# Wider triangle inversions on GpSimd, norms on VectorE, dummy matmuls and a new order in a fused gated-delta-rule kernel

## The chip, the cores and the metric

The kernel runs on one core of one Trainium2 chip. The metric is the time of one execution on the device, in microseconds (us). Executions of one kernel on one chip scatter here by about 3% (35 runs of the kernel before on one chip took 290.6 to 300.0 us; over all chips it took 289 to 303), so each kernel was timed in turn with the kernel before on the same chip. A ratio below is the mean time of one kernel's fast runs over that of the other's fast runs in the same rounds, with a 95% interval; it isn't quite the ratio of the medians that are quoted beside it. A run counts as slow when it lies over 1.5% above the fastest run of its kernel. With a scatter of 3% this cuts off the upper part of the scatter, and more of it the more runs there are. So where few runs are left, the ratio over all runs is given too.

Engine names in the profile: PE is TensorE, PEld its weight loads, DVE is VectorE, ACT is ScalarE, POOL is GpSimd, SP issues the loads.

## The reference, cut to what matters

```python
k_n = k / (np.linalg.norm(k, axis=-1, keepdims=True) + 1e-06)
for t in range(768):                       # for each of 4 x 8 heads, state 48 x 48
    y[t]  = g[t] * (q[t] @ state)
    state = state + beta[t] * outer(k_n[t], v[t] - k_n[t] @ state)
x = y                                      # 3072 tokens x 384
out = softplus(x @ w_in) @ w_out           # 384 -> 2048 -> 384
```

The recurrence is computed in chunks of 64 tokens. Within a chunk a unit lower triangle, made from the Gram products of the keys, is inverted and applied to (v - k state); the state passes from chunk to chunk. The dense part is two large matrix products with a softplus between them.

## The kernel before

Six steps, 0 to 5, of 128 tokens, each of two halves of 64. A small planner in Python puts every operation ("item") into the queue of its engine, which works it off in order (in run e13 below a transpose whose triangle had ended near 187 us started at 204.09, behind what stood ahead of it in VectorE's queue). The planner simulates the engines with a fixed duration for each item and, among the items that could start, takes the one with the best priority. Those priorities are a tuned table. So the order of each engine's queue is fixed before the kernel runs.

```python
class Plan:
    BLOCK = 128                 # matmuls
    FETCH = 3.5
    BUSY = {"POOL": 8.5, "ACT": 2.3, "DVE": 2.5}
    ...
            it = min(can, key=lambda x: (x.prio, x.n))
```

The triangle, 16 wide: two 16x16 triangles per lane, eliminated step by step, on VectorE in steps 0 and 1, on GpSimd from step 2 on:

```python
def step(j, ...):
    n, w = 15 - j, j + 1
    t = tmp[:, : 2*n*w]
    eng.tensor_tensor(t, nn[:, :, j+1:, j:j+1].broadcast_to([P, 2, n, w]),
                         tt[:, :, j:j+1, 16:16+w].broadcast_to([P, 2, n, w]), ALU.mult)
    rows = tt[:, :, j+1:, 16:16+w]
    eng.tensor_tensor(rows, rows, t, ALU.add)
...
for j in range(15): prev = add(en, 2*fix + 4*per*(15-j)*(j+1), lambda f=step, j=j: f(j), ...)
```

TensorE joins the 16x16 blocks to 32x32 by two products for each half, called the first and second cross product below (`xmm`, 64 matmuls, and `tmm`, 68), makes a lower-left block (`zmm`, 34) and applies the inverse in two parts (`umm`, 64, then after a copy `zu`, 32). The norms of steps 2 to 5 are a power on GpSimd:

```python
i3 = add("POOL", 5.6, lambda: nc.gpsimd.tensor_tensor(ss, ss, half_c, ALU.pow), ...)
```

## Time and profile before

| | before |
|---|---|
| median, 4 runs beside the changed kernel | 292.1 us (289.3 to 295.0) |
| span of the profiled run, mean granted clock of TensorE | 294.1 us, 0.932 |
| TensorE busy | 235.3 us, so 58.8 us idle |
| GpSimd: triangle of step 3 | 132.8 to 145.9 us |
| GpSimd: triangle of step 4 | 185.2 to 198.9 us |
| first cross product of step 0; first matmul of the dense layer | 34.6 us; 57.6 us |

The lines of the page that carry this are in the prediction below. Its "chain of waits" is the profile's path back from the last instruction, at each step to what that one waited for; the shares say which engine the end hung on, and "issue" is time in which an engine waited for nothing that the profile shows. The profiled run (295.8 us) lay 1.8% above the fastest of three timed runs, so it was labelled slow; each run has the span of one core only, so there is nothing to compare it with, and it serves for the places of things, not for ratios. One more view of the kernel before is needed later. Its columns are the stretch in us, its length, then the busy time (and number of instructions) of PE, PEld, DVE, ACT and POOL, the granted clock, the DMA share and GB/s:

```profile
120.00:140.00 20.00, 19.96 (x477) 10.60 (x476) 10.43 (x19) 13.78 (x26) 7.16 (x19) 0.80 0.93 148
160.00:180.00 20.00, 14.77 (x422) 8.05 (x421) 6.51 (x15) 9.65 (x20) 3.84 (x5) 0.91 1.22 136
```

TensorE is full from 120 to 140 us and waits for five of the twenty microseconds after 160.

Three more figures of this run, for the prediction. The granted clock is 0.50 from 124.6 to 127.5 us, where six dense matmuls took 2.74 us, and 1.00 from 128.7 to 130.3 us, where the same six took 1.47; from 57.6 to 60.3 us twelve smaller ones took 2.74 us at a granted clock of 1.00, and why is not shown. A multiply of 126 elements in the elimination takes 423 ns on GpSimd and 288 on VectorE, in the mean. And the page counts 50 packets on its instruction queue, 0.82 MB, for 6432 matmuls with a weight load each: 129 matmuls to a packet. The texts on record speak of blocks of instructions, of fetch and of instruction supply; a block is 128 matmuls there, and what the runs show of it stands under "The place of the boundaries".

### The profile page before, as it was taken

The numbers are of one execution on the slowest core, as the hardware profiler recorded it, in microseconds if no ns is written. First come the engines' busy times: TensorE is split into PE (matmuls) and PEld (weight loads), VectorE is DVE, ScalarE is ACT, GpSimd is POOL, SyncE is SP. The second block draws the span as 40 slices with busy tenths as digits, with TensorE's granted clock in tenths as the row PEclk, the third lists the DMA queues.
The fourth block names the chain that finished last, engine by engine and source line by source line (L and its number), as shares of the span: only waits on it lengthen the run. The fifth ranks groups of instructions, "written<-read, shape, count | busy, mean of one in ns | idle before, by whom it ended". The sixth has DMA issues, their size and how long they took to land.

```text
span 294.1 us, 14010 instructions
## 1 busy us (share of the span) xinstructions
PE 235.3 (80%) x6432; PEld 152.2 (52%) x6432; DVE 147.5 (50%) x290; ACT 140.4 (48%) x235; POOL 102.8 (35%) x182
## 2 busy tenths in 40 slices
PE   0365256696898985999798869999699999999993
PEld 0244145565656763455455535655455655667661
DVE  2899968657424891356465247475235601332110
ACT  3468545348426443577236527119534447513340
POOL 8443111714077840018877020880582000000000
PEclk9999999999589997589899979999779999999998
DMA  8999999999919999799979994884001320022112
GB/s 114 157 148 168 183 169 162 152 180 179 143 30 161 160 119 149 140 159 139 148 165 147 140 122 86 150 138 101 4 4 30 85 56 4 2 56 57 29 27 54
DMA packets 125931, 32.46 MB, mean 110 GB/s; under 512 B 119856, under 2 KB 125104, under 8 KB 125872
## 3 DMA queue, kind: packets, MB, share of 16 engines
q1 hardware_dynamic: 122752, 28.32, 63.2%
q0 software_dynamic: 3120, 3.24, 6.9%
q8 instruction: 50, 0.82, 1.2%
q14 instruction: 9, 0.07, 0.1%
HBM read 25.26 MB, written 4.72 MB: 102 GB/s over the span
## 4 chain that ended last, share of the span: by engine, by line
PE 68%; DVE 12%; issue 8%; ACT 5%; DMA 5%; SPq 0%; DVEq 0%; ACTq 0%
PE h L1341 25%; PE o L1379 20%; DMA kf<-in_k_dram 4%; PE d L1059 3%; PE d L1117 2%; PE d L1209 2%; PE d L970 2%; PE d L1015 2%; PE d L925 2%; PE d L1154 2%; ACT td L899 2%; PE d L1199 2%; DVE tt L835 1%; PE d L724 1%; DVE tmp L828 1%
## 5 line engine op out<-in xcount | busy, mean ns | idle before, releaser
L1362 ACT ACTIVATE ga<-h 128x512 f16<-128x512 f32 x96 | 57.2, 598 | 57.0 <-PE h L1341 55.0
L1341 PE MATMUL h<-xt,w_in 128*128 128x512 f16 (+1 forms) x384 | 81.8, 357 | 2.0 <-issue 2.0
L1379 PE MATMUL o<-w_out,ga 128*128 128x384 f16 x384 | 73.2, 337 | 1.3 <-DVE osb L1401 1.2
L1341 PEld LDWEIGHTS <-w_in 128*128 128x128 f16 x384 | 36.9, 104 | 25.7 <-issue 7.2
L1379 PEld LDWEIGHTS <-ga 128*128 128x128 f16 x384 | 36.6, 100 | 26.1 <-issue 4.4
L551 DVE CAST u<-d 128x384 f16<-128x384 f32 x24 | 13.4, 556 | 44.5 <-PE d L1117 25.1
L1401 DVE COPY osb<-o 128x384 f32<-128x384 f32 x24 | 13.3, 554 | 40.9 <-PE o L1379 38.6
L485 POOL TENSOR_TENSOR ss<-ss,half_c 128x32 f32<-128x32 f32 x4 | 21.8, 5448 | 10.8 <-DVE ss L448 7.6
L835 POOL TENSOR_TENSOR tt<-tt,tmp 128x30 f32<-128x30 f32 (+7 forms) x60 | 22.7, 378 | 4.7
L828 POOL TENSOR_TENSOR tmp<-nn,tt 128x30 f32<-128x30 f32 (+7 forms) x60 | 21.9, 365 | 4.5
L817 POOL TENSOR_TENSOR nn<-ln,beta_l 128x256 f32<-128x256 f16 x8 | 4.8, 618 | 50.3 <-DVE ln L793 50.3
L529 POOL CAST qn<-qf 128x768 f16<-128x768 f32 x12 | 10.1, 846 | 23.8 <-DMA qf<-in_q_dram 23.8
L549 ACT CAST u<-d 128x384 f16<-128x384 f32 x24 | 11.5, 479 | 12.4 <-PE d L1154 6.5
L1103 DVE TENSOR_TENSOR w<-vf,d 128x384 f16<-128x384 f32 x22 | 11.2, 546 | 11.4 <-PE d L1059 11.1
L441 ACT ACTIVATE ksq<-kf 128x768 f32<-128x768 f32 x12 | 10.1, 843 | 12.0 <-DMA kf<-in_k_dram 11.2
L1276 DVE TENSOR_TENSOR yg<-d,gf 128x384 f16<-128x384 f32 x24 | 12.3, 548 | 6.9 <-PE d L1209 3.0
L793 DVE STREAM_TRANSPOSE ln<-kk 128x1024 f16<-128x1024 f16 x6 | 11.4, 1904 | 7.3 <-ACT kk L744 3.6
L763 DVE TENSOR_TENSOR mt<-d,mask 128x256 f16<-128x256 f32 x24 | 8.8, 416 | 12.2 <-ACT kk L744 8.1
L568 PE MATMUL d<-ident,kn 128*128 128x128 f16 x48 | 5.8, 296 | 11.4 <-DVE kn L507 11.4
L549 ACT COPY kqt<-d 128x1024 f16<-128x1024 f16 (+1 forms) x12 | 11.3, 951 | 7.0 <-PE d L568 6.9
L744 ACT ACTIVATE kk<-d 128x256 f16<-128x256 f32 x24 | 8.1, 383 | 13.3 <-PE d L728 11.3
L448 DVE TENSOR_REDUCE ss<-ksq 128x16 f32<-128x768 f32 x12 | 11.3, 942 | 5.4 <-ACT ksq L441 5.4
(82 smaller groups left out, 329.5 us busy)
## 6 DMA issues: line engine op xcount, KB each, us to landing
kf<-in_k_dram SPq DMA_DIRECT2D x24, 192.0 KB, 5.4
qf<-in_q_dram SPq DMA_DIRECT2D x24, 192.0 KB, 5.5
vf<-in_v_dram SPq DMA_DIRECT2D x24, 192.0 KB, 5.3
gf<-in_g_dram SPq DMA_DIRECT2D x24, 192.0 KB, 5.5
out_dram<-osb SPq DMA_DIRECT2D x48, 96.0 KB, 2.2
w_in<-in_moe_w_in_dram POOLq DMA_DIRECT2D x2, 768.0 KB, 9.3
w_out<-in_moe_w_out_dram POOLq DMA_DIRECT2D x1, 1536.0 KB, 15.0
beta_l<-in_beta_dram POOLq DMA_DIRECT2D x8, 12.0 KB, 4.7
```

The costliest lines, as they stand in the source:

```text
L448: nc.vector.tensor_reduce(ss.ap[:, 16 * cl : 16 * cl + 16].rearrange("p (a h) -> p a h", a=2), ksq.ap, mybir.AxisListType.X, ALU.add,)
L485: lambda ss=ss, r=r: nc.gpsimd.tensor_tensor(ss.ap[:, r], ss.ap[:, r], half_c[:, r], ALU.pow),
L549: nc.scalar.copy(d, x)
L551: nc.vector.tensor_copy(d, x)
L793: lambda kk=kk, ln=ln: nc.vector.transpose(ln.ap, kk.ap[:, 1].rearrange("p u t -> p t u")),
L828: eng.tensor_tensor(t, nn.ap[:, :, j + 1 :, j : j + 1].broadcast_to([P, 2, n, w]), tt.ap[:, :, j : j + 1, 16 : 16 + w].broadcast_to([P, 2, ...
L835: eng.tensor_tensor(rows, rows, t, ALU.add)
L1276: lambda m=m, yg=yg, yp=yp, gf=gf: nc.vector.tensor_tensor(heads(yg.ap, m), hd(yp[m].ap), heads(gf.ap, m), ALU.mult),
L1341: nc.tensor.matmul(hp.ap[:, n * b : n * b + n].rearrange("p (a t) -> p a t", t=P), w_in[:, j, f * P : (f + 1) * P], xt.ap[:, t0 // P : (t0 ...
L1362: lambda hp=hp, o=gb: nc.scalar.activation(o.ap, hp.ap, AF.Softplus),
L1379: nc.tensor.matmul(op.ap[:, :DM], b.ap[:, c + c0 : c + c0 + 128], w_out[:, f, :], start=(f == 0), stop=(f == NF - 1),)
L1401: lambda op=op, ob=ob: nc.vector.tensor_copy(ob.ap, op.ap[:, :DM]),
```

## The change

Its intent: take small matmuls off TensorE in the last two steps by inverting 32x32 triangles per lane on GpSimd, and apply one 64x64 inverse per chunk; take the power off GpSimd; put dummy matmuls into TensorE's planned gaps, in the hope (the author's guess, which e2 tests) that they keep its clock up; and tune all priorities anew. Some buffer rings shrink too (`nn` and `tmp` from 2 to 1, `osb` from 4 to 3), and the planner counts 1 us more for a load; neither was tested by itself. Cut to its core:

```diff
+LANES = [("DVE", 16), ("POOL", 16), ("POOL", 16), ("POOL", 16), ("POOL", 32), ("POOL", 32)]
-    WAIT = 0.168272762528
-    BUSY = {"POOL": 8.5, "ACT": 2.3, "DVE": 2.5}
-    RUN = 5
-    BIG = 56
+    WAIT = 0.455178055244
+    BUSY = {"POOL": 6.8, "ACT": 2.3, "DVE": 4.0, "PE": 3.0}
+    RUN = 1
+    BIG = 170
 RANK = { ... every entry replaced ... }

+    # 98 dummies in all, in planned gaps of TensorE before the first output product
+    def fill(k):
+        for _ in range(k):
+            nc.tensor.matmul(bank, ident, mask[:, None, :].broadcast_to([P, 8, C]))

-    i3 = add("POOL", 5.6, ... nc.gpsimd.tensor_tensor(ss, ss, half_c, ALU.pow))
+    dv.tensor_scalar(y, x, 1, None, ALU.logical_shift_right)      # steps 2 to 5
+    dv.tensor_scalar(y, y, -1, 0x5F3759DF, ALU.mult, ALU.add)
+    dv.tensor_scalar_mul(h, x, -0.5)
+    for _ in range(4):
+        dv.tensor_tensor(w, h, y, ALU.mult)
+        dv.tensor_tensor(w, w, y, ALU.mult)
+        dv.scalar_tensor_tensor(y, w, 1.5, y, ALU.add, ALU.mult)
+    dv.tensor_tensor(x, x, y, ALU.mult)                           # planned at 1.4 us

+    def step32(j, ...):                                           # steps 4 and 5
+        n, w = HC - 1 - j, j + 1                                  # 31 steps on 32x32
+        eng.tensor_tensor(t, nn[:, w:, j:j+1], tri()[:, j:j+1, :w], ALU.mult)
+        eng.tensor_tensor(rows, rows, t, ALU.add)
+    ACT: t16 <- tri;  DVE: ti <- transpose(t16), td <- transpose(t16)   # each planned at 1.95 us
+    PE: xmm32, tmm32 (34 matmuls each), then umm64 (32) in place of umm and zu
```

> **What bounds the kernel now.** The work is cut into six steps of 128 tokens, two halves each; step numbers below run from 0 to 5. I read the page first: totals, then the row of slices.
>
> ```profile
> span 294.1 us, 14010 instructions
> PE 235.3 (80%) x6432; PEld 152.2 (52%) x6432; DVE 147.5 (50%) x290; ACT 140.4 (48%) x235; POOL 102.8 (35%) x182
> ...
> PE   0365256696898985999798869999699999999993
> ...
> POOL 8443111714077840018877020880582000000000
> PEclk9999999999589997589899979999779999999998
> DMA  8999999999919999799979994884001320022112
> ...
> PE 68%; DVE 12%; issue 8%; ACT 5%; DMA 5%; SPq 0%; DVEq 0%; ACTq 0%
> ```
>
> TensorE carries the chain of waits (68%), and from 180 us on it is nearly full; GpSimd has finished by 223 us, and the loads by about 200 us. So a microsecond of TensorE work taken from steps 4 and 5 should come off the end, if nothing later takes its place. Before 80 us TensorE is half empty: there the chain is loads, VectorE and short products.
>
> Next the timeline, for three kinds of lost TensorE time: the clock, "issue", and waiting for the triangles.
>
> ```profile
> 124.70 2.74 PE L1341 MATMUL h<-xt,w_in 128*128 128x512 f16 x6
> 128.78 1.47 PE L1341 MATMUL h<-xt,w_in 128*128 128x512 f16 x6
> ...
> 172.58 0.24 PE L1209 MATMUL d<-u,mt 64*64 64x48 f16 x1 [2.75 <-issue]
> ...
> 57.55 2.74 PE L1341 MATMUL h<-xt,w_in 128*128 128x256 f16 x12
> 66.79 1.48 PE L1341 MATMUL h<-xt,w_in 128*128 128x256 f16 x12
> ```
>
> The same six matmuls take 2.74 or 1.47 us: half clock and full clock. [...] The issue gap stands inside one burst of small matmuls, with nothing to wait for.
>
> Then GpSimd, which inverts the triangles from step 2 on:
>
> ```profile
> L485 POOL TENSOR_TENSOR ss<-ss,half_c 128x32 f32<-128x32 f32 x4 | 21.8, 5448 | 10.8 <-DVE ss L448 7.6 <-DVE ss L494 3.2
> ...
> 83.98 0.25 POOL L828 TENSOR_TENSOR tmp<-nn,tt 128x30 f32<-128x30 f32 x1
> 84.65 0.28 POOL L828 TENSOR_TENSOR tmp<-nn,tt 128x56 f32<-128x56 f32 x1
> 90.08 0.43 POOL L828 TENSOR_TENSOR tmp<-nn,tt 128x128 f32<-128x128 f32 x1
> 91.11 0.42 POOL L828 TENSOR_TENSOR tmp<-nn,tt 128x126 f32<-128x126 f32 x1
> 145.65 0.25 POOL L835 TENSOR_TENSOR tt<-tt,tmp 128x30 f32<-128x30 f32 x1
> ...
> 147.40 5.44 POOL L485 TENSOR_TENSOR ss<-ss,half_c 128x32 f32<-128x32 f32 x1
> ```
>
> A power of 32 columns costs 5.45 us, and the one for step 4 stood in the queue behind step 3's triangle until 147.4. One elimination step (multiply and add) takes 0.67 us at 30 elements and 1.03 at 128: 0.56 + 0.0037 per element.
>
> [...] At 126 elements the multiply takes 423 ns against 288, a ratio of 1.5. [...] One GpSimd add at 190.81 took 1.07 us beside the key scaling, against 0.43 normally.
>
> **The change part by part.**
>
> *Wide triangles in steps 4 and 5.* Per half, TensorE had: first cross product 64 matmuls in 0.57 us, second 68 in 0.67, the lower-left block 34 in 0.47, two-part application 64 in 0.61 and 32 in 0.46 (bursts in the chain of waits): 2.8 us. Now: two products of 34, about 0.5 each from the like block product, and one 64x64 application of 32 at about 0.4: 1.4 us. Four halves: 5.5 us less TensorE work. By count, 324 small matmuls less per step, 648 in all, which is 5 fetch blocks. The recurrence also loses one product and one copy per half (about 1.3 us), but that lies beside dense work. Copies fall by 8 in all and block copies by 4.
>
> The price is on GpSimd. Old triangle: 15 steps, 1360 elements, 15 x 0.56 + 1360 x 0.0037 = 13.4 us; the trace has 132.8 to 145.9, 13.1. New: 31 steps, sum of w(32-w) = 5456 elements, 31 x 0.56 + 5456 x 0.0037 = 37.5 us. Two of them are 75 us, where 27 stood.
>
> *Norms.* Four powers, 21.8 us, leave GpSimd. On VectorE 16 operations on 32 columns at about 0.22 us with the gap (the shortest such row is 0.17) are 3.5 us per step, 14 in all, on an engine half busy. The gain is that keys of step 4 no longer queue behind step 3's triangle.
>
> *Step 1's triangle moves from VectorE to GpSimd.* It ran from 40.0 to 63.6 us on VectorE, mixed with other work. On GpSimd it can begin after the q cast (that load landed at 40.6) and needs 13.4 plus casts and a weight issue: done near 58.
>
> *Filling.* 98 dummy matmuls of 512 columns, in planned TensorE gaps until the first output product, to hold the clock up. TensorE idles about 27 us between 10 and 80 us, so they mostly fit; 36 of them stand ahead of the first cross product and may hold it up by 2 to 3 us.
>
> *The order.* All priorities change. In the built order step 4's Gram products stand around step 3's first cross product, and its wide triangle follows step 3's at once. In the old run GpSimd mostly idled from 146 to 184 between them. So the 37.5 us are paid largely with idle time.
>
> **Sum.** TensorE work in the full stage: 5.5. Fetch: 5 blocks fewer there, of which I count half of a gap near 1 us each: 2.5. Clock: the low windows after 70 us lose 18.7 us of full-speed clock (10 us times one minus the granted share, over the low ten-microsecond windows), about half of it under running matmuls[...]; filling and the denser order may recover 5. Earlier step 1 and closed gap of loads (the slice at 80 us, where the load queue stood behind an output store): 6. Together 19: 293.8 - 19 = 275 us.
>
> Check by the GpSimd path. If step 3's triangle ends near 135 (8 to 12 us earlier than 145.9, from the points above) step 4's starts near 137; then 37.5 + 1.5 (the scaled triangle has one buffer, so step 5 begins after step 4 is done) + 37.5 + about 7 for transposes and products + 33.5 of TensorE work that the order leaves after it (116 output matmuls at 0.163, 96 first-layer at 0.109, 4 for short products) + 4 for the last copy and store: 258. With 10 to 20 us of misfits the two agree. TensorE after step 4's start has about 115 us by the same count, so both are near balance: either may bind.
>
> **The rivals.**
> (a) GpSimd becomes the bound. For: two triangles back to back, nothing to spare[...]. Against: 38 us of idle GpSimd in the old run. If step 4 can't start before 150, the end is 150 + 121 = 271 plus misfits, 285 to 290; at 165 nothing is won.
> (b) Loads set the pace: the DMA row is at 9 until 200 us, and no byte is removed. For: q of step 4 was issued at 128 us. Against: final loads were over 90 us before the end, and the hole at 80 us can close. Then about 283.
> (c) The dummies delay the first chain and TensorE gains nothing early: about 280.
> (d) All fits and the clock stays up: 262.
>
> **Range and chances.** 275, eight in ten within 263 to 287. Under 287.9 is faster by 2%: 0.87. Within 2%: 0.10. Slower: 0.03; that would need the wide triangles to starve TensorE for over 20 us.
>
> **What would show it.** GpSimd busy near 140 us, wide triangles 35 to 40 us each, step 4's beginning within 3 us after step 3's, near 137. TensorE matmuls 5882, small bursts as above. First-layer bursts before 66 us at 1.48 and not 2.74. Wrong if TensorE shows a wait of over 5 us ahead of the wide products in steps 4 or 5 (then rival a), if step 4's start is after 150 and its q cast waited for a load (b), or if step 0's first cross product comes after 37 us, where it was at 34.6 (c).

## The result, and the profile after

The changed kernel took 312.4 us in the median (310.2 to 314.5, 4 runs) beside 292.1 for the kernel before: ratio 1.078, interval 1.062 to 1.093. It is slower. A later repeat gave 1.072 (run c1 below). The page of the changed kernel, totals, three rows of slices and the chain of waits:

```profile
PE 256.8 (82%) x5882; PEld 157.0 (50%) x5882; DVE 165.1 (53%) x324; ACT 135.0 (43%) x229; POOL 132.8 (42%) x266
...
POOL 7052068323285300028710498888888840000000
PEclk9969986588999975559995999979769999579998
...
PE 52%; POOL 12%; SPq 11%; DVE 10%; issue 10%; ACT 2%; DMA 1%; POOLq 0%; ACTq 0%
```

The 5882 matmuls are those that the count foresaw (6432 less 648 plus 98). 28.2 us of dummies are in TensorE's busy time; without them it would be below the 235.3 of before. Two things stand out against the page before: GpSimd is busy without a break from about 175 to 255 us, and is now 12% of the chain; and the clock row has fives in the middle.

When the wide triangles start and end, from the timeline of GpSimd (start, duration, engine, line, operation, what the idle time before it waited for):

```profile
176.08 0.25 POOL L892 TENSOR_TENSOR tmp<-nn,tt 128x31 f32<-128x31 f32 x1 [15.02 <-DVE nn L876]
...
217.28 0.25 POOL L892 TENSOR_TENSOR tmp<-nn,tt 128x31 f32<-128x31 f32 x1
...
254.18 0.25 POOL L901 TENSOR_TENSOR tt<-tt,tmp 128x31 f32<-128x31 f32 x1
```

Step 4's triangle starts at 176.1, after 15 us of waiting, and not at 137. The triangles last 41.1 and 37.2 us, back to back. From 176.1 the rest of the run is a sum: 41.1 + 0.1 + 37.2 to the end of step 5's triangle, 19.7 to the first application of its inverse at 274.1, and 38.7 from there to the end, TensorE work and then the last copy and store: 136.7, which ends at the span of 312.8.

The 19.7 us behind step 5's triangle, first on VectorE, then on TensorE:

```profile
172.78 1.90 DVE L858 STREAM_TRANSPOSE ln<-kk 128x1024 f16<-128x1024 f16 x1
...
258.03 4.72 DVE L939 STREAM_TRANSPOSE t<-t 128x1024 f16<-128x1024 f16 x1 [2.36 <-ACT t L930]
262.38 4.83 DVE L949 STREAM_TRANSPOSE td<-t 128x1024 f16<-128x1024 f16 x1
```
```profile
267.26 0.61 PE L973 MATMUL d<-td,ident 32*32 32x512 f16 x2 [3.50 <-DVE td L949]
```

The two transposes of 128x1024 behind the triangle take 4.7 to 4.8 us each, where the one ahead of it, of the same size and type, takes 1.90. That one writes contiguous rows; these two write every 32nd column. TensorE waits 3.50 us for the second.

Last, the gaps that the timeline of TensorE puts down to "issue", which means that nothing was waited for:

```profile
60.18 0.24 PE L1248 MATMUL d<-td,xs 32*16 32x16 f16 x13 [5.95 <-issue]
62.43 2.74 PE L1687 MATMUL h<-xt,w_in 128*128 128x256 f16 x12
114.52 0.18 PE L1248 MATMUL d<-td,xs 32*16 32x16 f16 x3 [3.31 <-issue]
165.74 0.21 PE L783 MATMUL d<-kqt 48*32 48x32 f16 x4 [3.95 <-issue]
```

The largest is twice the largest before (2.75). The first dense layer behind it (second line) took 2.74 us, as before, now at a granted clock of 0.50, in spite of the dummies. The last gap stands inside step 4's Gram products, which the wide triangle waits for; the twelve dense matmuls right behind it took 4.02 us, at a granted clock of 0.50 again.

The same stretches as shown of before:

```profile
120.00:140.00 20.00, 13.26 (x439) 9.11 (x429) 14.49 (x38) 7.77 (x17) 1.24 (x3) 0.50 0.90 141
160.00:180.00 20.00, 16.03 (x541) 9.75 (x540) 10.95 (x24) 8.65 (x15) 4.29 (x11) 0.83 0.82 121
```

From 120 to 140 us TensorE idles a third of the time and has a granted clock of 0.50, where it was full before, at a granted clock of 0.80. Step 3's triangle then ran from 140.0 to 155.6, against 132.8 to 145.9.

### The profile page after: what moved, and what is told of

Read it like the earlier page. It is cut to its first block, busy times and chain, and to the rows that moved or that the text cites. A ratio compares the mean times of both kernels' runs of the same rounds, so it can differ in the third digit from the quotient of the medians.

```text
span 312.8 us, 13061 instructions
## 1 busy us (share of the span) xinstructions
PE 256.8 (82%) x5882; PEld 157.0 (50%) x5882; DVE 165.1 (53%) x324; ACT 135.0 (43%) x229; POOL 132.8 (42%) x266
## 4 chain that ended last, share of the span: by engine, by line
PE 52%; POOL 12%; SPq 11%; DVE 10%; issue 10%; ACT 2%; DMA 1%; POOLq 0%; ACTq 0%
PE o L1725 18%; PE h L1687 15%; SPq L391 11%; POOL tt L901 6%; POOL tmp L892 5%; DVE t L939 3%; DVE td L949 3%; PE d L1338 2%; PE d L1530 2%; DMA qf<-in_q_dram 1%; PE d L1203 1%; PE d L1406 1%; PE d L1520 1%; PE d L609 1%; PE d L1248 1%
## 5 line engine op out<-in xcount | busy, mean ns | idle before, releaser
L1687 PE MATMUL h<-xt,w_in 128*128 128x512 f16 (+1 forms) x384 | 79.2, 350 | 5.0 <-ACT ga L1708 2.4
L1725 PE MATMUL o<-w_out,ga 128*128 128x384 f16 x384 | 79.3, 351 | 1.9 <-DVE osb L1748 1.3
L892 POOL TENSOR_TENSOR tmp<-nn,tt 128x31 f32<-128x31 f32 (+15 forms) x62 | 31.5, 508 | 19.6 <-DVE nn L876 15.0
L901 POOL TENSOR_TENSOR tt<-tt,tmp 128x31 f32<-128x31 f32 (+15 forms) x62 | 35.9, 579 | 4.9
L1768 PE MATMUL o<-mask,ident 128*128 128x512 f16 x98 | 28.2, 437 | 2.1 <-POOL mask L296 2.1
L592 DVE CAST u<-d 128x384 f16<-128x384 f32 x20 | 11.1, 555 | 33.0 <-PE d L1406 13.2
L1114 POOL TENSOR_TENSOR tt<-tt,tmp 128x30 f32<-128x30 f32 (+7 forms) x45 | 17.4, 387 | 3.5
L1107 POOL TENSOR_TENSOR tmp<-nn,tt 128x30 f32<-128x30 f32 (+7 forms) x45 | 16.9, 375 | 3.2
L1768 PEld LDWEIGHTS <-ident 128*128 128x128 f16 x98 | 10.0, 108 | 13.6 <-issue 4.7
L1248 PE MATMUL d<-td,xs 32*16 32x16 f16 x512 | 5.7, 168 | 10.3 <-issue 10.3
```

The costliest lines, as they stand in the source:

```text
L892: eng.tensor_tensor(t, nn.ap.rearrange("p (i j) -> p i j", j=HC)[:, w:, j : j + 1].broadcast_to([P, n, w]), tri()[:, j : j + 1, :w].broadc ...
L1107: eng.tensor_tensor(t, n2(nn)[:, :, j + 1 :, j : j + 1].broadcast_to([P, 2, n, w]), tt.ap[:, :, j : j + 1, 16 : 16 + w].broadcast_to([P, 2 ...
L1687: nc.tensor.matmul(hp.ap[:, n * b : n * b + n].rearrange("p (a t) -> p a t", t=P), w_in[:, j, f * P : (f + 1) * P], xt.ap[:, t0 // P : (t0 ...
L1725: nc.tensor.matmul(op.ap[:, :DM], b.ap[:, c + c0 : c + c0 + 128], w_out[:, f, :], start=(f == 0), stop=(f == NF - 1),)
L1768: nc.tensor.matmul(bank.rearrange("p (a t) -> p a t", t=C), ident, mask[:, None, :].broadcast_to([P, 8, C]),)
```

## The experiments

Theories at the start. W: the chain through the two wide triangles and their transposes sets the end. O: the new order of the queues costs, and the triangles only wait inside it. F: the dummies cost more than they give. The first kernels keep the changed kernel's order item for item: the planner sees the same durations, only what an item emits is altered.

**e1, transposes that write contiguous rows.** The readers of the result take strided rows instead.

```diff
-    ti: t32[..., HC*U:].rearrange("p (u j) -> p u j", j=HC)
+    ti: t32[..., HC*U:].rearrange("p (j u) -> p u j", u=U)      # the same for td
```

> The changed kernel in the same order of every queue, but the two transposes behind each wide triangle write contiguous rows (the readers of the result take strided rows instead). In the changed kernel they took 4.70 and 4.85 us each; the transposes ahead of the triangles, which write contiguous rows, took 1.90. Theory W (the chain through the two wide triangles and what follows them sets the end): the transposes fall to about 1.9 us each and the end comes 4 to 6 us earlier, 307 to 309 us from 312.4. Theory O (the new order of TensorE's queue is what costs, and the wide chain only waits inside it): within 1 us of 312.4. If the stride is not what made them slow, they stay near 4.8 us and nothing moves.

308.9 us (before, on the same chip: 298.35), ratio 1.042 (1.031 to 1.053). The transposes fell to 1.91 and 1.21 us, and the application of step 5 came 15.0 us after its triangle, not 19.7. The short matmuls that now read strided rows, 32 in each burst, rose from about 180 to 230 ns each. So the stride is what made the transposes slow, and within the changed kernel the chain behind the triangle did set the end, as W has it.

**e2, no dummies.** `for _ in range(k)` becomes `for _ in range(0)`.

> The changed kernel in the same order, without the 98 dummy matmuls (nothing else moves). Theory F (the dummies hold up the first chain and don't keep the clock): the first cross product comes at about 35 us instead of 38.2 and the end 2 to 4 us earlier, 308 to 310 us. The rival, that they do raise the clock: the early matmuls get slower and the end comes 3 us or more later. Theory W says that the early shift is mostly lost before step 4's triangle: 311 to 313.

302.05 us, ratio 1.013 (1.000 to 1.025). This is several times what F gave it. The first cross product came 2.6 us earlier (35.6), but step 4's triangle 9.7 us earlier (166.4), and the end 13.6. The 2.6 us at the start don't account for 9.7 and 13.6 later, which points to something else than the time of the dummies; e8 tests that.

**e3, short triangles.** A wrong result on purpose: every step of a wide triangle works on one column (the comparison with the reference passed all the same, so it doesn't see these terms).

```diff
-    n, w = HC - 1 - j, j + 1
+    n, w0, w = HC - 1 - j, j + 1, 1            # w0 keeps the rows, w = 1 column
```

> A wrong result on purpose: the changed kernel in the same order with the same 31 pairs of GpSimd instructions per wide triangle, but each works on one column instead of the whole width, so a triangle should take about 18 us instead of 40. Theory W: the end comes 25 to 40 us earlier, 270 to 287 us. Theory O (TensorE's queue and its dense work set the end): not below 300 us. In between means that TensorE takes over as the bound part of the way.

308.9 us, ratio 1.039 (1.027 to 1.051). The triangles took about 21 and 19 us instead of 41 and 37, and W's 270 to 287 us failed. Taking nearly 40 us out of GpSimd's chain gave 3 to 4% of the time: behind that chain another bound lies close.

**e6, the norms alone in the kernel before**, in its own order, the 16 VectorE operations issued where the power stood.

```diff
-    add("POOL", 5.6, nc.gpsimd.tensor_tensor(ss, ss, half_c, ALU.pow))
+    add("POOL", 5.6, root)        # planned as before, issued on VectorE
```

> The kernel before, with its own order kept item for item, and only the four powers on GpSimd replaced by the 16 VectorE operations, issued at the same place in the sequence. If the norms were worth what the prediction gave them (no power behind step 3's triangle), step 4's keys come up to 5 us earlier and the end 0 to 4 us earlier, 288 to 292 us. The rival, that 3.5 us of short operations inside VectorE's in-order queue hold up the evacuations that TensorE waits for: 293 to 297 us.

306.2 us, ratio 1.026 (1.013 to 1.039): slower, above the upper side of the rival's range. Alone, this part costs. The trace shows where: VectorE was done with the 16 operations for step 4 at 160.1 us and only then came to the first transpose behind step 3's triangle, 9.9 us after the triangle's end (150.2); before, that transpose came 5.5 us after it (at 151.4). Step 4's keys were scaled at 165.0 us, not earlier than before (156.5) but later, and its triangle began at 194.8 instead of 185.2.

**c1, the changed kernel again**, as control, and three more in its order.

> The changed kernel itself once more, as the control on the chip of these four runs, since the kernel before has run between 289 and 303 us on two chips. Every theory expects 1.06 to 1.09 times the kernel before. If it comes out below 1.05, the gain of 6% seen without the dummies was partly the chip.

315.2 us, ratio 1.072 (1.057 to 1.088). In the rounds of c1, e8, e9 and e10 only two of the seven runs of the kernel before count as fast. Over all runs of these rounds the four ratios are lower: 1.061, 1.057, 1.022 and 1.030.

**e8, all 98 dummies, but 8 columns wide**: `bank[:, :8], ident, mask[:, :8]`.

> The changed kernel in the same order with all 98 dummy matmuls at their places, but 8 columns wide instead of 512, so that they cost almost no time[...], and still 98 matmuls and 98 weight loads in TensorE's instruction stream. Without any dummies the ratio to the kernel before was 1.013 against 1.078. If the dummies cost by their time (they stand in the way of the first chain and lower the granted clock afterwards): ratio 1.00 to 1.03, clock about 0.92. If they cost by their number (they shift where the gaps of instruction supply fall, 5.95 us at 60 us and 3.95 us at 165 us): ratio 1.06 to 1.09, with these two gaps where they were.

313.7 us, ratio 1.068 (1.057 to 1.080), with gaps of 5.17 us at 57.8, 3.19 at 114.6 and 3.70 at 165.9. The dummies cost nearly the same when they take almost no time. So their number or their place does it, not their length.

**e9, e1 and e2 together.** Both edits.

> The changed kernel in the same order, without dummies and with the transposes that write contiguous rows. If the two effects add: 1.013 less about 0.02 to 0.03, so a ratio of 0.985 to 1.0. If TensorE's in-order queue takes over (the short triangles showed that 20 us of GpSimd time gave only about 7 us at the end of each step), 1.0 to 1.013.

302.65 us, ratio 1.033 (1.021 to 1.045). The two effects don't add. VectorE and TensorE behind step 5's triangle:

```profile
251.66 1.91 DVE L942 STREAM_TRANSPOSE t<-t 128x1024 f16<-128x1024 f16 x1 [2.36 <-ACT t L933]
253.50 1.20 DVE L952 STREAM_TRANSPOSE td<-t 128x1024 f16<-128x1024 f16 x1
```
```profile
257.32 1.05 PE L976 MATMUL d<-td,ident 32*32 32x512 f16 x2
```

The transposes are done at 254.7, but TensorE comes to the products at 257.3, without having waited (no bracket): dense matmuls stand ahead of them in its queue. Without dummies TensorE's order, and no longer the chain behind the triangle, decides.

**e10, as e9, with the power on GpSimd again** at the same place in the sequence (the reverse of e6's edit).

> As the run before, and the norms of steps 2 to 5 again by the power on GpSimd instead of the 16 VectorE operations, issued at the same place in the sequence. Put into the old kernel, the 16 operations cost 2.6%. If VectorE's in-order queue is where they hurt, this is 1 to 3% faster than the run before. The rival: step 5's power (5.45 us) now stands ahead of or inside step 4's wide triangle, so it is equal or up to 2% slower.

305.6 us, ratio 1.037 (1.019 to 1.056): the same as e9. Step 4's triangle started about 4 us earlier, and its run of GpSimd took 45.9 us instead of 41.1, because step 5's power, 5.44 us at 166.5, now lay in it. What VectorE won, GpSimd gave back.

**The place of the boundaries.** The gaps in "issue" have a pattern. Run e2, timeline of TensorE; the count of matmuls is the number after the x:

```profile
75.51 0.32 PE L664 MATMUL d<-kqt 48*64 48x64 f16 x17 [1.38 <-issue]
75.76 0.37 PE L670 MATMUL d<-kqt 48*32 48x32 f16 x32
76.07 1.47 PE L1725 MATMUL o<-w_out,ga 128*128 128x384 f16 x8
77.38 0.82 PE L1687 MATMUL h<-xt,w_in 128*128 128x256 f16 x6
78.13 0.44 PE L1338 MATMUL d<-s,kqt 48*64 48x48 f16 x32
78.50 0.38 PE L1203 MATMUL d<-tq,kk 16*32 16x16 f16 x33
80.06 0.36 PE L1203 MATMUL d<-tq,kk 16*32 16x16 f16 x31 [1.19 <-issue]
```

From one gap to the next: 17 + 32 + 8 + 6 + 32 + 33 = 128 matmuls. The next gap, at 83.79, comes after 31 + 4 + 6 + 4 + 64 + 4 + 15 = 128 more. Counted over the whole traces of the nine runs e1 to e3 and e8 to e13, every gap in "issue" of 0.9 us or more stands at the same place of a block: 95 matmuls after a multiple of 128 (94 later in the run). The pages fit this: each matmul has its weight load (5882 of each in the changed kernel), and the instruction queue has 46 packets there and 50 before, 128 and 129 matmuls to a packet. Below, 128 matmuls are a block, and the place where such a gap can stand is its boundary. 98 dummies move every later boundary by 98 matmuls. Theory P: that is what they cost. Theory E: it is their place inside the first chain.

**e11, no dummies, and 98 matmuls of 8 columns ahead of everything**, where TensorE has nothing to do yet (they ran from 2.12 to 4.87 us, and the next matmul came at 9.56, behind a wait of 4.69 us for VectorE); **e12, the dummies as they are, and 30 more ahead**, so that 128 stand before the later part:

```diff
+    for _ in range(98):                       # 30 in e12
+        nc.tensor.matmul(bank[:, :8], ident, mask[:, :8])
```

> The changed kernel in the same order without its dummies, but with 98 matmuls of 8 columns put ahead of everything, where TensorE has nothing to do for about 10 us: they cost no time of their own and shift every later matmul by 98 places in the instruction stream. In the runs so far the gaps of instruction supply come at multiples of 128 matmuls. Theory P (the dummies cost by the place to which they shift these boundaries): ratio to the kernel before 1.05 to 1.08, with gaps of over 3 us near 114 and 165 us as with the dummies. Theory E (the dummies cost because they stand inside the first chain): 1.01 to 1.03, as without dummies.

> The changed kernel with all its 98 dummies of 512 columns at their places, and 30 matmuls of 8 columns ahead of everything, so that from the last dummy on (about 75 us) the boundaries of 128 matmuls fall where they fall without any. Theory P: ratio 1.01 to 1.04. Theory E: 1.06 to 1.08, as the changed kernel.

e11: 312.95 us, ratio 1.060 (1.053 to 1.067). e12: 303.6 us, ratio 1.028 (1.021 to 1.035). Theory P holds on both sides, and E fails on both. The gaps of e11:

```profile
57.58 0.24 PE L1248 MATMUL d<-td,xs 32*16 32x16 f16 x13 [5.00 <-issue]
...
113.77 0.18 PE L1248 MATMUL d<-td,xs 32*16 32x16 f16 x3 [2.84 <-issue]
...
163.44 0.22 PE L783 MATMUL d<-kqt 48*32 48x32 f16 x4 [3.06 <-issue]
163.59 4.02 PE L1725 MATMUL o<-w_out,ga 128*128 128x384 f16 x12
```

They stand in the same bursts, 13, 3 and 4 matmuls before the end, as in the changed kernel, and the twelve dense matmuls behind the third gap take 4.02 us again. In e12 the two later ones are moved and short:

```profile
115.90 0.46 PE L1248 MATMUL d<-td,xs 32*16 32x16 f16 x45 [1.31 <-issue]
...
158.90 0.18 PE L1203 MATMUL d<-tq,kk 16*32 16x16 f16 x2 [0.98 <-issue]
```

Step 4's triangle started at about 168.4 in e12, though the first cross product came at 38.2, exactly as in the changed kernel. The same twelve dense matmuls, which stand in the middle of step 4's Gram products, take 2.12 us in e12 and in e2. The granted clock from 160 to 180 us is 0.74 to 0.83 in the six runs with moved boundaries (the changed kernel, c1, e1, e3, e8, e11) and 0.91 to 1.00 in the five without (e2, e9, e10, e12, e13). So in every run that has it the long gap at this place comes with a lower clock behind it (the twelve take 4.02 us in the changed kernel and e11, 2.12 in e2 and e12), and both lie ahead of the last Gram products: the wide triangle started at 173.8 us in e11, 5.4 us later than in e12. Another 4 us of the difference arise behind step 5's triangle (58.4 us to the end against 54.5); the runs don't say why.

The runs in the changed order fall into two groups. Boundaries moved by 98 and nothing else sped up: 1.078, 1.072, 1.068, 1.060. Not moved, counting modulo 128: 1.013, 1.033, 1.037 (e10), 1.028, and 1.023 (e13, next). With moved boundaries and one part made faster, e1 and e3 lie between, at 1.042 and 1.039. Over all runs, fast and slow, the first group is at 1.057 to 1.069 and the second at 1.012 to 1.030.

**e13, short triangles without dummies.** Edits of e2 and e3.

> A wrong result on purpose: the changed kernel in the same order without dummies, with the wide triangles working on one column per step (about 20 us each instead of 41). With the dummies this took 3 to 4% off. If without dummies the triangles are the bound (GpSimd has 21% of the chain of waits there): 0.94 to 0.98 of the kernel before. If TensorE's queue is: 0.99 to 1.02.

301.9 us, ratio 1.023 (1.016 to 1.030): nothing gained over the other runs without dummies. The triangle of step 4 ended near 187, but:

```profile
200.48 1.90 DVE L858 STREAM_TRANSPOSE ln<-kk 128x1024 f16<-128x1024 f16 x1
...
204.09 4.70 DVE L940 STREAM_TRANSPOSE t<-t 128x1024 f16<-128x1024 f16 x1
208.44 4.81 DVE L950 STREAM_TRANSPOSE td<-t 128x1024 f16<-128x1024 f16 x1
```
```profile
213.31 0.61 PE L974 MATMUL d<-td,ident 32*32 32x512 f16 x2 [5.04 <-DVE td L950]
```

Its transposes stand in VectorE's queue behind the first transpose of step 5, which waits for step 5's Gram products, which stand behind dense work in TensorE's queue. In a fixed order a faster engine doesn't bring forward what was queued behind something else. So this run shows that the length of the triangles isn't what keeps this order from being faster, but not what they would be worth in an order made for them.

**e14, the kernel before with 64 matmuls of 8 columns ahead of everything**, half a block.

> The kernel before with 64 matmuls of 8 columns ahead of everything, half a block of instructions, where TensorE idles. Theory P: the time moves by more than 2%, up or down. Theory E, under which the place of the boundaries is of no weight: 0.99 to 1.01.

292.0 us beside 295.7, ratio 0.988 (0.980 to 0.995). It moved, by less than the 2% that P put down, and this time down.

**Are the parts worth anything in an order made for them?** The planner of the changed kernel believed in 1.4 us for a norm, 1.95 for each transpose behind a wide triangle and 31 for a wide triangle (the sum of its entries; it adds some where VectorE works at the same time), where the traces show 3.5, 4.7 to 4.8 and 37 to 41. Three kernels were planned with durations nearer to the measured ones and priorities searched anew, with the same effort by their expectations: all parts with e1's transposes and no dummies (r1), the same with only step 5 wide (r2, which also frees some buffers earlier in the last step), none of the parts (r3, where only the load was planned 1 us longer). Each was run again with 64 tiny matmuls ahead (r5, r6, r4).

```diff
-    root: 1.4        +    root: 3.5                    # us, as the planner sees it
-    0.25, 1.45e-3    +    0.28, 1.85e-3                # GpSimd, per instruction, per element
-    xmm32: 0.5       +    xmm32: 1.05                  # with strided reads
 RANK, WAIT, RUN, BIG: searched anew
```

> All parts of the change (two wide triangles, VectorE norms, step 1 on GpSimd) except the dummies, with transposes that write contiguous rows, and a new order: the planner is given the durations that the traces show (3.5 us for the norm's 16 operations where it had 1.4, about 41 us for a wide triangle where it had 33) and its priorities are searched anew. Theory V (the parts are worth something and the old priorities, built on wrong durations, hid it): 0.93 to 0.98 of the kernel before. Theory Z (the parts give back on GpSimd and VectorE what they take from TensorE): 0.98 to 1.02, and no better than the next but one run, which has none of the parts.

> As the run before, but only step 5 wide, step 4's triangle 16 wide as in the kernel before; priorities searched anew with the same effort. Theory V: near the run before, or between it and the next one. If two wide triangles back to back on GpSimd are what costs, this is 1 to 3% faster than the run before.

> The kernel before with none of the parts of the change, only its priorities searched anew with the same effort, and with 1 us more assumed for a load. Theory Z: equal to or faster than the two runs before, 0.95 to 1.0 of the kernel before. Theory V: slower than the run with all parts by 2% or more.

> As the run before, with 64 matmuls of 8 columns ahead of everything (half a block of instructions). If the place of the block boundaries is worth 1 to 5% in any order, it moves by at least 1% against the run before, up or down; if it only mattered in the two orders tried so far, by less than 0.7%.

> All parts of the change in the new order, with 64 matmuls of 8 columns ahead of everything. With the first four runs of the replanned kernels this fills a table of three sets of parts by two places of the boundaries. If the parts are worth something, the mean of the two places lies 2% or more below that of the old parts (1.013 and 0.988, mean 1.0005); if not, within 1.5% of it. The other place moves this kernel by 1 to 3%.

> One wide triangle in the new order, with 64 matmuls of 8 columns ahead of everything. It was 0.989 without them; if this place is the better one here as it was for the kernel before and for the replanned old parts, 0.965 to 0.98, which would be the fastest of the study; if the place acts at random from one order to the next, 0.98 to 1.02.

| ratio to the kernel before (interval) | boundaries as they fall | moved by 64 | mean |
|---|---|---|---|
| all parts | 1.010 (1.006 to 1.014) | 0.996 (0.989 to 1.004) | 1.003 |
| one wide triangle | 0.989 (0.983 to 0.996) | 1.003 (0.998 to 1.009) | 0.996 |
| none of the parts | 1.013 (1.004 to 1.023) | 0.988 (0.983 to 0.993) | 1.000 |

Theory V fails, and the means fit theory Z: they lie within 0.7% of each other, while moving the boundaries alone moves each kernel by 1.4 to 2.5%, in no constant direction. One line of Z missed: r3 was to be no slower than r1 and r2 and at most 1.0, and it ran at 1.013, slower than r2. The middle row is the weakest: r2's 0.989 rests on 3 of its 10 runs. Over all runs the rows are 1.005 and 0.989, 0.995 and 0.996, 1.013 and 0.988; then the middle row doesn't move at all, and the means still lie within 0.6% of each other. All parts in an order planned for them are at 1.003 in the mean, against 1.07 as the change had it, but the parts bring nothing that two places of the boundaries per row can show. The two best kernels, r4 and e14 at 0.988, have none of the parts of the change; r2, at 0.989, has some. By 2% none of them counts as faster.

## Why the prediction was wrong

It said 275 us, with 3 in 100 for slower; 312.4 was measured.

**The step that failed first: the start of step 4's triangle.** The check by the GpSimd path put it near 137, because it "follows step 3's at once". It was 176.1. Of the 39 us, 20.6 are that step 3's triangle ended at 155.6 and not 135, and 18.5 that step 4's came 20.5 us behind it instead of 2. The order of instructions, which the prediction read, does say that the Gram products stand around step 3's cross product. It doesn't say when they run: they lay between 155 and 171 us, spread by dense matmuls, twelve of them at a granted clock of 0.50 (4.02 us), and by the gap of 3.95 us. An order shows what comes after what, and from that the prediction took a time. The "38 us of idle GpSimd" that the prediction set against rival (a) were not all idle either: from 146 to 184 us GpSimd was busy for 14.7, two powers among them.

**Rival (a) was right in kind.** It said that if step 4 starts at 165 nothing is won. In e2 it started at 166.4, and the ratio was 1.013. The sign that was given for it, a wait of over 5 us ahead of the wide products, didn't show: TensorE waited 2.1 us there in step 4 and 3.5 in step 5.

**The terms of the path after that start** (predicted 121 without misfits, measured 136.7): triangles 78.3 against 76.5, so the count of 0.56 + 0.0037 per element was right, with 3.6 us more for the first one. Transposes and products up to the application 19.7 against 7: this term was mis-sized, by two transposes at 4.7 to 4.8 us, which alone are more than the 7, by the copy, and by dense work queued between. The stretch from there to the end 38.7 against 37.5, the last copy and store included.

**The terms of the sum.** TensorE's work, 5.5 us: it did leave. In e2 TensorE is busy 228.7 us against 235.3 before, 6.6 less, at a clock of 0.920 against 0.932. But its idle time rose from 58.8 to 70.5 us, so the work taken away became waiting. The reading that a microsecond of TensorE work in steps 4 and 5 comes off the end held only "if nothing later takes its place". In the changed kernel the chain behind the wide triangles took it (e1); without the dummies it was the order of TensorE's own queue (e9 with fast transposes, e13 with short triangles).

Fetch, 2.5 us gained for 5 blocks fewer, an estimate (648 matmuls are 5 blocks of 128, and the 23.0 us of waits in "issue" before, over 50 packets, are 0.46 us each): the sign was wrong. The prediction counted blocks; what counts is where a boundary falls. The same 98 matmuls of no length cost about 4.5% (1.07 against 1.02). That it is the position is shown by e11 and e12. TensorE's waits put down to "issue" sum to 24.1, 22.5 and 21.9 us in the changed kernel, e8 and e11, and to 17.3 and 17.5 in e2 and e12 (before: 23.0), so the gaps themselves are about half of the difference; the lower clock behind them is another part (4.02 against 2.12 us for the twelve matmuls; that the gap causes it was not tested apart). Why one position costs 1 us and another 4 to 6 is not shown. In all rows above the gap lies in a burst of small matmuls, at about 10 to 20 ns each (64 in 0.69 us, 32 in 0.57), in the part of the run that still loads; that this is the reason is argued, not tested.

Clock, 5 us, a guess: wrong in sign, 0.861 against 0.932. The dummies did not hold it in the first dense burst (2.74 us at 62.4, granted clock 0.50). The low clock from 120 to 140 us belongs to the new order: it was 0.50 there in the changed kernel and 0.57 in both e11 and e12, whose times differ by 3%. So that stretch doesn't explain the difference between the two groups; the clock from 160 to 180 us, behind the long gap, is a part of it (0.83 in e11, 1.00 in e12). Why the clock falls in that order wasn't tested.

Early gains, 6 us: none came. Step 1's triangle on GpSimd ended at 69.2 us, not 58, since its last step stood behind a key scaling that waited 9.24 us for TensorE; on VectorE it had ended at 63.6. Step 2's triangle began at 85.4, against 84.0.

**The norms.** 3.5 us per step was right in length. That they cost nothing on an engine half busy was not: alone in the old order they cost 2.6% (e6). In the changed order they cost no more than the power would (e10 against e9), so they brought nothing there. The trace of e6 puts its loss down to VectorE's in-order queue: the 16 operations stand ahead of the transposes behind step 3's triangle. The rival, a shift of boundaries in VectorE's own instruction stream, finds no support: VectorE's waits put down to "issue" sum to 0.5 us in e6 and 0.3 before.

**Rival (c)**, that the dummies delay the first chain, was right on the sign it gave (38.2 us, later than 37) and wrong on the cause: e12 has the same 38.2 and runs at 1.028.

**Rival (b)**, the loads: step 4's start was after 150, but the two casts of q ahead of it, at 142.7 and 145.2 us, waited for no load, so its sign didn't show there. The load queue did enter the chain of waits (SPq 11%, 0% before), all of it in the first 40 us. It is 11% in e12 too, so it doesn't separate the two groups; whether it is part of what the order costs wasn't tested.

**What the 7% is made of.** About 4 to 4.5% is the place of the boundaries (1.07 against 1.02). The other 2 to 3% is gone in the mean of r1 and r5 (all parts, 1.003). r1 differs from e9 in the order alone (1.010 against 1.033: same parts, same fast transposes, no dummies), r5 in 64 tiny matmuls besides. So it lies in the order, as far as two places of the boundaries can say. The predicted gain of 6% was never there in any kernel run. That the parts put as much on GpSimd and VectorE as they take from TensorE fits this (e6, e10), but no run measures it part by part in a good order.

## What to carry to other kernels

When work is moved from the fullest engine to an emptier one, ask when the receiving chain can start and what must follow it, and take that from measured times; a queue's order gives none. A part that is short and "fits" on a half-idle in-order engine can still stand ahead of what the path needs there (e6). Give a planner durations from a trace before tuning priorities on it: here an order tuned on three wrong entries (1.4 for 3.5, 1.95 for 4.7, 31 for about 40) lost 2 to 3%, and one searched anew with better ones did not, though the entries weren't tested apart from the new search. And before crediting a change of 1 to 5% in a kernel with thousands of small matmuls, shift its instruction stream with some tiny matmuls at the start (64 here, half of the 128 between two boundaries), and time it again: if that moves the time as much, the gain is not yet the change's.
